# Turning the mixer's activations by DMA instead of on TensorE: six of eight batches of an attention and token/channel-mixer kernel on Trainium2

## The chip, the cores and the metric

The kernel runs on one core of one Trainium2 chip. The metric is the device time of one launch in microseconds (us), the median over the runs shown. The profile is one execution taken by the hardware profiler; its rows name the engines PE (TensorE matmul), PEld (TensorE weight load), DVE (VectorE), ACT (ScalarE), POOL (GpSimd) and SP (SyncE, which here issues most DMAs).

## The reference, cut to what matters

Eight batches, eight heads, 576 tokens of 64 channels per head. Heads 0 to 3 attend to the last 32 tokens, heads 4 to 7 to every fourth of the last 128. The heads' outputs, side by side, are the 576 x 512 matrix x of a batch. It is mixed along the tokens, added to itself, and mixed along the channels:

```python
scores = scale * np.matmul(q, k.transpose(0, 1, 3, 2))
scores = np.where(masks, scores, -1e9)
attn = softmax(scores)
x = heads_side_by_side(np.matmul(attn, v))
h = np.maximum(x.transpose(0, 2, 1) @ w_tok1, 0.0) @ w_tok2
u = x + h.transpose(0, 2, 1)
h2 = np.maximum(u @ w_ch1, 0.0) @ w_ch2
out = u + h2
```

The channel product `u @ w_ch1` sums over the 512 channels, so on TensorE u must lie with its channels on the partitions, while it is computed with its tokens there. u therefore has to be turned over: four channel blocks (cb) of 128, each 128 channels by 576 tokens.

## The kernel before, in words

All matmuls are in fp16. The order of the work is written by hand. `gen_main(b)` is the trunk of batch b: first the channel product `gp` (line 602: 12 row blocks x 2 token halves x 4 channel blocks, in the order 2, 0, 3, 1 of `CBS`, 288 columns each, with a relu into `gt`), then the output product `yp` (line 619: token blocks s = 0 to 3 of 128, each in two column halves of 12 matmuls with 256 columns). After each `yp` block VectorE adds u and writes `o32` (line 629), and SP stores it. Odd batches have one more block (line 639), the last 64 tokens ("the tail") of the batch and of the one before it. `gp` and `yp` share three PSUM banks in turn.

Between the pieces of the trunk of batch b, `interleave` puts the steps that prepare batches b+1 and b+2. Each step has a place on a clock that the generator keeps: every piece of the trunk and every step advances it by a number written beside it (0.65 for half a `yp` column half, 0.28 for one channel block turned over), and a step is emitted once the clock has passed its place. So a step with a later place comes later on every engine, and a step that is taken out lets more of the trunk go ahead of the steps behind it.

For batch b+1 the steps are `value_steps` (attention times values into `xn`), then `mix_steps`: `emit_h1`, `emit_u` (the second token product; VectorE adds `xn` to it and writes u in fp16 as `u16`, line 518, and the tail as `u16t`, line 528) and `emit_uT`. `emit_uT` (lines 530 to 551) turns one channel block: five TensorE transposes (four token blocks and the tail, lines 540, 542, 548, 549) into a PSUM bank, and one copy of 128 x 576 to the tile `uT`, by VectorE or ScalarE. Channel blocks 2 and 3 belong to the dilated heads, whose tokens lie sorted by their remainder of 4; there the copy also puts them back in natural order.

For batch b+2 the steps are casts by GpSimd (`cast_steps`), DMA transposes of q and k (`dma_steps`, line 336) and the copies of the turned blocks to their places (`place_steps`: `plain` on GpSimd, lines 358 and 360; `tails`, `dil` and `dil_k` on VectorE, lines 354, 355, 364, 369), and `score_steps`. For each of four pairs of heads `score_steps` emits three groups of score matmuls into the banks `sc`, `sc` and `sm`, with ScalarE's exponentials; then GpSimd multiplies the results by the mask, in a wide and a narrow product per pair (`mult`, line 113: `attp` for the two plain pairs, `attd` for the two dilated ones).

Every engine works through its own list in order, and SP through its list of DMAs. Below, "the hand-over into batch b" is the moment at which TensorE goes from the last `yp` matmul of batch b-1 to the first `gp` matmul of batch b.

Of the kernel before, what the change touches and what calls it, by code (L numbers as in the profile page):

```python
# [9 lines left out]
FP16 = mybir.dt.float16  # L10
FP32 = mybir.dt.float32
AF = mybir.ActivationFunctionType
ALU = mybir.AluOpType
# [3 lines left out]
S = 576  # L17
# [3 lines left out]
DM = 512  # L21
# [16 lines left out]
CBS = (2, 0, 3, 1)  # L38
# [31 lines left out]
def kernel(  # L70
# [11 lines left out]
    nc = tc.nc  # L82
# [4 lines left out]
    def fixed(name, shape, dtype=FP16):  # L87
        return sb.tile(shape, dtype, tag=name, bufs=1, name=name)
# [29 lines left out]
    ident = const[:, 0:128]  # L118
# [33 lines left out]
    w4 = [w4a[:, i] for i in range(NMB)]  # L152
    idle = fixed("idle", [128, 512])

    def emit_fixed():
# [346 lines left out]
    def emit_u(b, s, h1):  # L502
        p = bank("fl", 3, f"up_{b}_{s}")
        if s < 4:
            summed = b == 1 and s in (0, 2)
            for half in range(2):
                c = slice(256 * half, 256 * half + 256)
                if summed:
                    nc.tensor.matmul(out=p[:, c], lhsT=ident, rhs=xn[b][:, s, c], start=True, stop=False)
                for jb in range(2):  # L510
                    nc.tensor.matmul(  # L511
                        out=p[:, c], lhsT=w2p[jb][:, s] if half else w2[jb][:, 128 * s:128 * s + 128],
                        rhs=h1[jb][:, c], start=(jb == 0 and not summed), stop=(jb == 1))
            t = sb.tile([128, DM], FP16, tag="u16", bufs=8, name=f"u16_{b}_{s}")
            if summed:
                nc.scalar.copy(out=t, in_=p)
            else:
                nc.vector.tensor_tensor(out=t, in0=p, in1=xn[b][:, s], op=ALU.add)  # L518
            u16[(b, s)] = t
        else:  # L520
            odd = b % 2
            c0 = 448 if odd else 512
            for jb in range(2):
                nc.tensor.matmul(out=p, lhsT=w2[jb][:, c0:c0 + 128], rhs=h1[jb],  # L524
                                 start=(jb == 0), stop=(jb == 1))
            rows = slice(64, 128) if odd else slice(0, 64)
            t = u16t[b // 2]
            nc.vector.tensor_tensor(out=t[rows], in0=p[rows], in1=xn[b][rows, 4], op=ALU.add)

    def emit_uT(b, cb):  # L530
        odd = b % 2
        c = slice(128 * cb, 128 * cb + 128)
        p = bank("fl" if b or cb % 2 == 0 else "main", 3, f"tpu_{b}_{cb}", FP16)
        tl = u16t[b // 2][:, c]
        t = sb.tile([128, S], FP16, tag="ut", bufs=5, name=f"uT_{b}_{cb}")
        eng = nc.scalar if cb == 2 or (b and cb == 3) else nc.vector
        if cb < 2:
            m0, t0, c0 = (128, 0, 64) if odd else (0, 512, 0)
            for s in range(4):
                nc.tensor.transpose(out=p[:, m0 + 128 * s:m0 + 128 * s + 128],  # L540
                                    in_=u16[(b, s)][:, c], identity=ident)
            nc.tensor.transpose(out=p[:, t0:t0 + 128], in_=tl, identity=ident)
            copy(eng, t, p[:, c0:c0 + S])
        else:
            grid = p[:, 0:4 * RS].rearrange("p (r i) -> p r i", i=RS)
            m0, t0, c0 = (32, 0, 16) if odd else (0, 128, 0)
            for s in range(4):
                nc.tensor.transpose(out=grid[:, s, m0:m0 + 128], in_=u16[(b, s)][:, c], identity=ident)  # L548
# [27 lines left out]
    def mix_steps(b, t_h1, t_h1b, t_u, t_uT, du=1.0):  # L576
        if b % 2 == 0 and b // 2 not in u16t:
            u16t[b // 2] = sb.tile([128, DM], FP16, tag="u16t", bufs=2, name=f"u16t_{b // 2}")
        h1 = [sb.tile([128, DM], FP16, tag="h1", bufs=4, name=f"h1_{b}_{jb}") for jb in range(2)]
        steps = []  # L580
        for half, at in ((0, t_h1), (1, t_h1b)):
            for jb in range(2):
                steps.append((at + 0.9 * jb, 0.55, lambda jb=jb, half=half: emit_h1(b, jb, half, h1[jb])))
        for i, s in enumerate((4, 0, 1, 2, 3)):
            steps.append((t_u + du * i, 0.44, lambda s=s: emit_u(b, s, h1)))
        for i, cb in enumerate(CBS):
            steps.append((t_uT + 0.9 * i, 0.28, lambda cb=cb: emit_uT(b, cb)))
        return steps

    def gen_main(b):  # L590
# [18 lines left out]
        for s in ((4, 0, 1, 2, 3) if odd else (0, 1, 2, 3)):  # L609
            p = bank("main", 3, f"yp_{b}_{s}")  # L610
            o32 = sb.tile([128, DM], FP32, tag="o32", bufs=4, name=f"o32_{b}_{s}")
            if s < 4:
                for half in range(2):
# [12 lines left out]
                    if last and s == 3:  # L626
                        nc.vector.tensor_tensor(out=o32[:, c], in0=p[:, c], in1=u16[(b, s)][:, c], op=ALU.add)
                    elif half:
                        nc.vector.tensor_tensor(out=o32, in0=p, in1=u16[(b, s)], op=ALU.add)  # L629
                    if half or (last and s == 3):  # L630
# [6 lines left out]
            else:  # L637
                for mb in range(NMB):
                    nc.tensor.matmul(out=p, lhsT=gt[(b // 2, mb)][:, 512:640], rhs=w4[mb],  # L639
                                     start=(mb == 0), stop=(mb == NMB - 1))  # L640
                    if mb in (3, 7):
                        yield 0.87
                nc.vector.tensor_tensor(out=o32, in0=p, in1=u16t[b // 2], op=ALU.add)
                nc.sync.dma_start(out=out[b - 1, 512:S, :], in_=o32[0:64])
# [41 lines left out]

    u16t[0] = sb.tile([128, DM], FP16, tag="u16t", bufs=2, name="u16t_0")

    def gate(t, src):
# [31 lines left out]
    nc.gpsimd.memset(u16t[0][64:128], 0.0)  # L721

# [50 lines left out]
    h1 = [sb.tile([128, DM], FP16, tag="h1", bufs=4, name=f"h1_0_{jb}") for jb in range(2)]  # L773
    for s in range(4):
        u16[(0, s)] = sb.tile([128, DM], FP16, tag="u16", bufs=8, name=f"u16_0_{s}")

    def u_half(s, half):
        p = bank("main" if half else "fl", 3, f"up_0_{s}_{half}")[:, 0:256]
        c = slice(256 * half, 256 * half + 256)
        rows = slice(0, 64) if s == 4 else slice(0, 128)  # L780
        t = u16t[0] if s == 4 else u16[(0, s)]
        summed = s in (0, 2)
# [6 lines left out]
        if summed:  # L789
            nc.scalar.copy(out=t[:, c], in_=p)  # L790
        else:
            nc.vector.tensor_tensor(out=t[rows, c], in0=p[rows], in1=xn[0][rows, s, c], op=ALU.add)

# [42 lines left out]
    for b in range(B):  # L836
# [64 lines left out]
```

## Time and profile before

| | |
|---|---|
| median of 3 runs | 300.8 us (300.75 to 302.64) |
| the profiled execution: its own time | 300.74 us |
| the profiled execution: span of the profile | 298.7 us |
| granted TensorE clock, mean | 0.997 |
| PE busy | 286.8 us, 3112 matmuls |
| DVE / ACT / POOL busy | 159.3 / 140.8 / 180.1 us |

The span runs from the first to the last instruction of the profile; what lies around it is the other 2.0 us of the execution's time. Busy time is the time in which an engine has an instruction under way. A number in square brackets in the timeline is idle time ahead of an instruction, with what ended it.

### The profile page before, as it was taken

To read this page: it belongs to the slowest core of one execution; us is meant where nothing else is said; L and a number is where in the kernel's file an instruction comes from. 1 tells how busy PE (TensorE), PEld (TensorE's weight loads), DVE (VectorE), ACT (ScalarE), POOL (GpSimd) and SP (SyncE) were. 2 spreads that over 40 slices of the span, in tenths; PEclk is the share of its full clock that TensorE was granted. 3 is DMA by queue.
4 is the path that set the end of the run, shared out by engine and by line. 5 is a ranking of instruction groups with operands and counts; after the bars stand their busy time and mean duration, and the time that the engine had idled before them with its cause. 6 is when DMAs were issued, how large, how long until landed. Compare 5 with 4: busy or idle time off the path is not lost.

```text
span 298.7 us, 7805 instructions
## 1 busy us (share of the span) xinstructions
PE 286.8 (96%) x3112; PEld 257.2 (86%) x3112; DVE 159.3 (53%) x357; ACT 140.8 (47%) x319; POOL 180.1 (60%) x244
## 2 busy tenths in 40 slices
PE   5789999998999999999999999999999999999995
PEld 2687999987987999899987999899988999899794
DVE  5875438756737965643645254644745264532122
ACT  2853436377652545455545536365554535304500
POOL 7882056429998899739992999449992930000000
PEclk9999999999999999999999999999999999999998
DMA  7999999966997999984599749964551220022023
GB/s 219 270 212 177 214 312 222 326 165 188 286 196 128 279 288 154 280 211 151 69 205 276 211 111 153 307 139 146 120 55 35 72 72 0 3 71 72 2 70 105
DMA packets 91443, 49.10 MB, mean 164 GB/s; under 512 B 59760, under 2 KB 90352, under 8 KB 91408
## 3 DMA queue, kind: packets, MB, share of 16 engines
q1 hardware_dynamic: 87168, 43.53, 59.7%
q0 software_dynamic: 2640, 3.91, 7.4%
q10 hardware_dynamic: 1600, 1.18, 1.3%
q8 instruction: 24, 0.39, 0.6%
q14 instruction: 11, 0.09, 0.1%
HBM read 37.04 MB, written 9.44 MB: 156 GB/s over the span
## 4 chain that ended last, share of the span: by engine, by line
PE 92%; DVE 3%; DMA 2%; ACT 1%; issue 1%; ACTq 0%; POOLq 0%
PE gp L602 31%; PE yp L619 28%; PE sc L393 4%; PE h1p L499 4%; PE up L511 4%; PE yp L639 3%; DMA const<-consts 2%; PE sm L393 1%; PE tpu L548 1%; PE av L469 1%; PE h1p L497 1%; PE av L480 1%; PE tpu L540 1%; PE up L524 1%; PE av L467 1%; PE sc L391 1%
## 5 line engine op out<-in xcount | busy, mean ns | idle before, releaser
L602 PE MATMUL gp<-uT,w 128*128 128x288 f16 x768 | 109.9, 286 | 0.7 <-ACT uT L101 0.6
L619 PE MATMUL yp<-w,gt 128*128 128x256 f16 x756 | 95.6, 273 | 0.0
L107 ACT ACTIVATE gt<-gp 128x288 f16<-128x288 f32 x138 | 56.6, 410 | 72.1 <-PE gp L602 65.9
L602 PEld LDWEIGHTS <-w 128*128 128x128 f16 x768 | 83.1, 113 | 8.2 <-issue 1.2
L619 PEld LDWEIGHTS <-gt 128*128 128x128 f16 x768 | 75.9, 106 | 3.7
L113 POOL TENSOR_TENSOR attp<-attp,const 128x1280 f16<-128x1280 f16 (+1 forms) x24 | 36.0, 1529 | 32.9 <-ACT attp L422 32.9
L629 DVE TENSOR_TENSOR o<-yp,u 128x512 f32<-128x512 f32 x31 | 21.3, 689 | 50.6 <-PE yp L619 44.2
L109 DVE TENSOR_SCALAR gt<-gp 128x288 f16<-128x288 f32 x54 | 24.6, 455 | 35.5 <-PE gp L602 33.5
L113 POOL TENSOR_TENSOR attd<-attd,const 128x1024 f16<-128x1024 f16 (+1 forms) x24 | 32.8, 1397 | 0.0
L113 DVE TENSOR_TENSOR xn<-av,rec 128x320 f16<-128x320 f32 x64 | 31.5, 491 | 2.2
L393 PEld LDWEIGHTS <-kt 128*128 128x128 f16 x272 | 22.5, 101 | 3.1 <-DVE kt L302 1.6
L103 POOL CAST c_q<-l_q 128x512 f16<-128x512 f32 x31 | 18.9, 613 | 6.4 <-DMA l_q<-in_q_dram 5.7
L413 ACT ACTIVATE attp<-sc 128x480 f16<-128x480 f32 x32 | 18.0, 572 | 9.5 <-PE sc L393 9.4
L518 DVE TENSOR_TENSOR u<-up,xn 128x512 f16<-128x512 f32 x26 | 17.9, 691 | 8.0 <-PE up L511 8.0
L360 POOL COPY qz<-qt 64x512 f16<-64x512 f16 x20 | 21.4, 1072 | 0.6
L442 ACT ACTIVATE attd<-sc 128x512 f16<-128x512 f32 x32 | 18.9, 597 | 5.3 <-PE sc L393 4.7
L488 DVE RECIPROCAL rec<-av 128x5 f32<-128x5 f32 x64 | 12.2, 191 | 14.3 <-PE av L475 7.2
L393 PE MATMUL sc<-qz,kt 128*128 128x160 f16 (+1 forms) x144 | 18.6, 228 | 1.3 <-DVE kt L302 1.3
L103 POOL CAST c_k<-l_k 128x512 f16<-128x512 f32 x29 | 18.0, 622 | 3.0 <-DMA l_k<-in_k_dram 1.3
L101 ACT COPY uT<-tpu 128x576 f16<-128x576 f16 x15 | 9.6, 640 | 16.3 <-PE tpu L549 16.3
L107 ACT ACTIVATE h<-h1p 128x256 f16<-128x256 f32 x28 | 10.7, 383 | 10.1 <-PE h1p L499 8.0
L639 PE MATMUL yp<-w,gt 128*128 128x512 f16 x48 | 12.0, 379 | 0.0
(131 smaller groups left out, 444.4 us busy)
## 6 DMA issues: line engine op xcount, KB each, us to landing
out_dram<-o SPq DMA_DIRECT2D x72, 128.0 KB, 2.5
l_q<-in_q_dram SPq DMA_DIRECT2D x15, 512.0 KB, 6.4
l_k<-in_k_dram SPq DMA_DIRECT2D x14, 512.0 KB, 7.4
l_vn<-in_v_dram SPq DMA_DIRECT2D x32, 128.0 KB, 6.7
l_vd<-in_v_dram SPq DMA_DIRECT2D x16, 256.0 KB, 3.9
w<-in_moe_w_ch_dram POOLq DMA_DIRECT2D x6, 512.0 KB, 7.6
lt<-in_q_dram SPq DMA_DIRECT2D x8, 128.0 KB, 4.4
l_vt<-in_v_dram SPq DMA_DIRECT2D x8, 128.0 KB, 4.3
```

What stands on the lines that cost most here:

```text
L103: eng.tensor_copy(out=out, in_=in_)
L107: nc.scalar.activation(out=out, in_=in_, func=AF.Relu)
L109: eng.tensor_scalar_max(out=out, in0=in_, scalar1=0.0)
L113: eng.tensor_tensor(out=out, in0=x, in1=y, op=ALU.mult)
L360: nc.gpsimd.tensor_copy(out=natural(qz[hp][halves[h], h, 0:512]), in_=qta[halves[h], hp].rearrange("p r m -> p m r"))
L393: nc.tensor.matmul(out=out, lhsT=lhsT, rhs=qz[hp][:, h, queries], start=hide is None, stop=True)
L413: nc.scalar.activation(out=blocks[:, h, 0:3, 0:BLK], in_=p[:, 0:3 * BLK].rearrange("p (b c) -> p b c", c=BLK), func=AF.Exp, scale=0.125)
L442: nc.scalar.activation(out=a[:, h, 0:DTL], in_=p, func=AF.Exp, scale=0.125)
L602: nc.tensor.matmul(out=p[:, 0:288], lhsT=w3[cb][:, 512 * (mb // 4) + mb % 4:512 * (mb // 4) + 512:4], rhs=uT[(b, cb)][:, 288 * sh:288 * sh ...
L619: nc.tensor.matmul(out=p[:, c], lhsT=gt[(b // 2, mb)][:, a0:m0 + 512:4] if half else gt[(b // 2, mb)][:, a0:a0 + 128], rhs=w4[mb][:, c], s ...
L629: nc.vector.tensor_tensor(out=o32, in0=p, in1=u16[(b, s)], op=ALU.add)
L639: nc.tensor.matmul(out=p, lhsT=gt[(b // 2, mb)][:, 512:640], rhs=w4[mb], start=(mb == 0), stop=(mb == NMB - 1))
```

## The change

From batch 2 on, u is no longer turned on TensorE. u of a batch is written into one tile of 128 x (4 channel blocks, 4 token blocks, 128). Two DMA transposes on SP's list turn it: the tail (4 blocks of 128 x 128, into `uTt`) and the four token blocks (16 blocks, into `uTm`), placed at 2.0 and 6.0 after the batch's first step of u. Then four VectorE copies bring the turned blocks into the tile `uTd` that `gp` reads: the tail of all channel blocks; channel block 2, whose tokens are read with a stride to put them in natural order; channel blocks 0 and 1 in one copy; and channel block 3, strided as well. They are placed 0.9 apart from 28.4 on (29.6 for batch 2), where the turning on TensorE began at 18.2 (22.2). Neither the DMA steps nor the copies advance the generator's clock. Batches 0 and 1 keep `emit_uT`. `uTm`, `uTt` and `uTd` are one buffer each, and GpSimd zeroes the second half of both tail tiles at the start instead of one. The views `u16(b, s)` and `blocks4` only reshape the operands of the other instructions.

```diff
+    uTm = fixed("utm", [128, 4, 4, 128])
+    uTt = fixed("utt", [128, 4, 128])
+    uTd = fixed("utd", [128, 4, S])
...
-    xn, u16, u16t, uT, gt = {}, {}, {}, {}, {}
+    xn, u16w, uT, gt = {}, {}, {}, {}
+    u16t = [fixed(f"u16t{i}", [128, 4, 128]) for i in range(2)] * 2
+
+    def u16(b, s):
+        if b not in u16w:
+            u16w[b] = sb.tile([128, 4, 4, 128], FP16, tag="u16", bufs=2, name=f"u16_{b}")
+        return u16w[b][:, :, s]
...
-            t = sb.tile([128, DM], FP16, tag="u16", bufs=8, name=f"u16_{b}_{s}")
             if summed:
-                nc.scalar.copy(out=t, in_=p)
+                nc.scalar.copy(out=u16(b, s), in_=blocks4(p))
             else:
-                nc.vector.tensor_tensor(out=t, in0=p, in1=xn[b][:, s], op=ALU.add)
-            u16[(b, s)] = t
+                nc.vector.tensor_tensor(out=u16(b, s), in0=blocks4(p), in1=blocks4(xn[b][:, s]), op=ALU.add)
...
+    def turned(b):
+        return b >= 2
+
+    def uT_dma(b, tail):
+        if tail:
+            nc.sync.dma_start_transpose(out=uTt, in_=u16t[b // 2].rearrange("p x c -> p (x c)"))
+        else:
+            nc.sync.dma_start_transpose(out=uTm.rearrange("p x s t -> p (x s) t"),
+                                        in_=u16w[b].rearrange("p x s c -> p (x s c)"))
+
+    def uT_place(b, i):
+        r0, m0, t0 = (64, 64, 0) if b % 2 else (0, 0, 512)
+        if i == 0:
+            for cb in range(4):
+                uT[(b, cb)] = uTd[:, cb]
+            nc.vector.tensor_copy(out=uTd[:, :, t0:t0 + 64], in_=uTt[:, :, r0:r0 + 64])
+        elif i == 1:
+            nc.vector.tensor_copy(out=uTd[:, 0:2, m0:m0 + 512], in_=uTm[:, 0:2].rearrange("p x s t -> p x (s t)"))
+        else:
+            nc.vector.tensor_copy(out=natural(uTd[:, i, m0:m0 + 512]), in_=uTm[:, i].rearrange("p r m -> p m r"))
...
-        for i, cb in enumerate(CBS):
-            steps.append((t_uT + 0.9 * i, 0.28, lambda cb=cb: emit_uT(b, cb)))
+        if turned(b):
+            for t, tail in ((2.0, True), (6.0, False)):
+                steps.append((t_u + t * du, 0.0, lambda tail=tail: uT_dma(b, tail)))
+            for i, x in enumerate((0, 2, 1, 3)):
+                steps.append((t_uT + 0.9 * i, 0.0, lambda x=x: uT_place(b, x)))
+        else:
+            for i, cb in enumerate(CBS):
+                steps.append((t_uT + 0.9 * i, 0.28, lambda cb=cb: emit_uT(b, cb)))
...
-            steps += mix_steps(2, 10.8, 14.6, 17.2, 22.2)
+            steps += mix_steps(2, 10.8, 14.6, 17.2, 29.6)
...
-                steps += value_steps(b + 1, 0.6, 1.1) + mix_steps(b + 1, 6.6, 10.6, 13.2, 18.2)
+                steps += value_steps(b + 1, 0.6, 1.1) + mix_steps(b + 1, 6.6, 10.6, 13.2, 28.4)
```

VectorE's list ahead of the hand-over into batch 3, before. `o32_2_s` is the output add of token block s of batch 2, `uT_3` the turned u of batch 3, `gt_0` the first relu of batch 3:

```order
L103 COPY uT_3_0_2456<-tpu_3_0_2455 128x576
L629 TENSOR_TENSOR o32_2_0_2429<-yp_2_0_2428,u16_2_0_1769 128x512
L103 COPY uT_3_1_2489<-tpu_3_1_2488 128x576
L629 TENSOR_TENSOR o32_2_1_2504<-yp_2_1_2503,u16_2_1_1783 128x512
L629 TENSOR_TENSOR o32_2_2_2564<-yp_2_2_2563,u16_2_2_1796 128x512
L629 TENSOR_TENSOR o32_2_3_2614<-yp_2_3_2613,u16_2_3_1814 128x512
```

The same place in the changed kernel (`utt`, `utm` and `utd` are the tiles `uTt`, `uTm` and `uTd`):

```order
L663 TENSOR_TENSOR o32_2_1_2433<-yp_2_1_2432,u16_2_1767 128x512
L663 TENSOR_TENSOR o32_2_2_2489<-yp_2_2_2488,u16_2_1767 128x512
L578 COPY utd_89<-utt_88 128x4x64
L582 COPY utd_89<-utm_87 128x512
L663 TENSOR_TENSOR o32_2_3_2544<-yp_2_3_2543,u16_2_1767 128x512
L580 COPY utd_89<-utm_87 128x2x512
L582 COPY utd_89<-utm_87 128x512
```

Two of the four copies now stand behind the add of the last token block, which needs the last `yp` of batch 2; the hand-over into batch 5 reads the same. The hand-overs into 4 and 6, here into 4, have the last two copies ahead of that add:

```order
L663 TENSOR_TENSOR o32_3_1_3034<-yp_3_1_3033,u16_3_2337 128x512
L578 COPY utd_89<-utt_88 128x4x64
L582 COPY utd_89<-utm_87 128x512
L663 TENSOR_TENSOR o32_3_2_3089<-yp_3_2_3088,u16_3_2337 128x512
L580 COPY utd_89<-utm_87 128x2x512
L582 COPY utd_89<-utm_87 128x512
L663 TENSOR_TENSOR o32_3_3_3147<-yp_3_3_3146,u16_3_2337 128x512
```

So has the one into batch 2, except that there the add of block 2 stands between the copy of channel blocks 0 and 1 and that of block 3. Into batch 7 all four copies stand behind the last add:

```order
L663 TENSOR_TENSOR o32_6_2_4673<-yp_6_2_4672,u16_6_4030 128x512
L663 TENSOR_TENSOR o32_6_3_4702<-yp_6_3_4701,u16_6_4030 128x512
L578 COPY utd_89<-utt_88 128x4x64
L582 COPY utd_89<-utm_87 128x512
L580 COPY utd_89<-utm_87 128x2x512
L582 COPY utd_89<-utm_87 128x512
```

Nothing stands between the last of these copies and the first relu of batch 7. On SP's list the large transpose of batch 3 comes behind the first load of v for batch 5:

```order
L191 DMA l_q_5_0_2315<-in_q_dram 128x4x256
L568 DMA_TRANSPOSE utt_88<-u16t1_91 128x4x128
L191 DMA l_k_5_0_2317<-in_k_dram 128x4x256
L191 DMA l_q_5_1_2316<-in_q_dram 128x4x256
L191 DMA l_k_5_1_2318<-in_k_dram 128x4x256
L208 DMA l_vn_5_2403<-in_v_dram 128x4x64
L570 DMA_TRANSPOSE utm_87<-u16_3_2337 128x16x128
L208 DMA l_vn_5_2403<-in_v_dram 128x4x64
```

Before, neither transpose stood there; the loads followed one another.

More of the change, by code (lines that the diff above doesn't have):

```diff
@@ L642, in gen_main @@
                         yield 0.87
[L643 removed]
+                nc.vector.tensor_tensor(out=blocks4(o32), in0=blocks4(p), in1=u16t[b // 2], op=ALU.add)
                 nc.sync.dma_start(out=out[b - 1, 512:S, :], in_=o32[0:64])
@@ L720 @@
             out=w2p[jb], in_=w2[jb][:, 0:512].rearrange("p (m r) -> p r m", r=4))
-    nc.gpsimd.memset(u16t[0][64:128], 0.0)
+    for i in range(2):
+        nc.gpsimd.memset(u16t[i][64:128], 0.0)
     warm(8)
@@ L789, in u_half @@
         if summed:
-            nc.scalar.copy(out=t[:, c], in_=p)
+            nc.scalar.copy(out=t, in_=blocks4(p))
         else:
-            nc.vector.tensor_tensor(out=t[rows, c], in0=p[rows], in1=xn[0][rows, s, c], op=ALU.add)
+            nc.vector.tensor_tensor(out=t[rows], in0=blocks4(p[rows]), in1=blocks4(xn[0][rows, s, c]), op=ALU.add)
     for jb in range(2):
```

22 lines of the change are left out of this document (9 added, 13 removed).

## The prediction

> **What bounds the kernel now.** I read the page first, then the windows between hand-overs, then the chain of waits.
>
> ```profile
> span 298.7 us, 7805 instructions
> PE 286.8 (96%) x3112; PEld 257.2 (86%) x3112; DVE 159.3 (53%) x357; ACT 140.8 (47%) x319; POOL 180.1 (60%) x244
> ```
>
> ```profile
> core 0: us, PE busy (x) PEld busy (x) DVE busy (x) ACT busy (x) POOL busy (x), PEclk, DMA share, GB/s
> ...
> 107.13:139.21 32.08, 32.08 (x357) 29.64 (x356) 16.60 (x40) 16.35 (x37) 25.04 (x31) 1.00 0.91 217
> 139.21:173.72 34.51, 34.51 (x372) 30.82 (x369) 17.27 (x41) 17.11 (x39) 28.73 (x34) 1.00 0.74 181
> ...
> 240.30:270.10 29.80, 29.80 (x313) 27.46 (x312) 14.83 (x33) 10.19 (x24) 1.30 (x2) 1.00 0.11 37
> ```
>
> The windows begin and end at hand-overs (into 2 at 107.13, into 3 at 139.21, into 4 at 173.72, into 7 at 270.1). From one to the next TensorE is busy for the whole window (32.08 of 32.08 us) at full clock, and no other engine is. So a matmul taken out there is worth its time, and every wait that TensorE gets is lost in full. The chain gives TensorE's pace:
>
> ```profile
> 262.33 7.86 PE yp L619 x72
> 270.19 11.76 PE gp L602 x96
> ```
>
> That is 0.109 us per `yp` matmul and 0.1225 per `gp` matmul.
>
> **What the change removes.** The timeline of TensorE around the turning of batch 3:
>
> ```profile
> 126.19 0.82 PE L619 MATMUL yp<-w,gt 128*128 128x256 f16 x6
> 126.85 0.39 PE L540 MATMUL tpu<-const,u 128*128 128x128 f16 x4
> 127.07 0.22 PE L542 MATMUL tpu<-const,u16t 128*128 128x128 f16 x1
> 127.13 0.82 PE L619 MATMUL yp<-w,gt 128*128 128x256 f16 x6
> ```
>
> From one `yp` group to the next are 0.94 us; the six `yp` matmuls take 0.655, so five transposes take 0.285, though each row shows 0.22 or more (matmuls overlap). Four blocks in six batches: 24 x 0.285 = **6.8 us** off TensorE. The copies out of PSUM that go too (two on DVE, two on ACT per batch) bring nothing, since neither engine bounds.
>
> **What it adds: copies between two SBUF tiles on VectorE.** The kernel has such copies already, in the same forms: line 364 dense, line 355 the tail, line 369 read with the stride. By line or tile, min/median/max, then the timelines of VectorE and GpSimd where the maxima lie:
>
> ```profile
> L364 DVE COPY qz<-qt x10: 407/416/2729, 98.1 to 228.8; 64x1024 f16<-64x1024 f16 x10
> L369 DVE COPY kt<-kr x10: 263/272/2685, 101.3 to 229.4; 128x128 f16<-128x128 f16 x10
> L355 DVE COPY kt<-tt x5: 226/226/977, 94.4 to 225.1; 128x256 f16<-128x256 f16 x5
> ```
>
> ```profile
> 98.10 3.17 DVE L364 COPY qz<-qt 64x1024 f16<-64x1024 f16 x2
> 101.30 2.99 DVE L369 COPY kt<-kr 128x128 f16<-128x128 f16 x2
> 104.20 1.27 DVE L629 TENSOR_TENSOR o<-yp,u 128x512 f32<-128x512 f32 x2
> ```
>
> ```profile
> 98.33 6.25 POOL L113 TENSOR_TENSOR attp<-attp,const 128x1280 f16<-128x1280 f16 x4 [1.94 <-ACT attp L422]
> 104.54 5.47 POOL L113 TENSOR_TENSOR attd<-attd,const 128x1024 f16<-128x1024 f16 x4
> ```
>
> ```profile
> L113 POOL TENSOR_TENSOR attp<-attp,const 128x1280 f16<-128x1280 f16 x12 | 31.4, 2615 | 32.9 <-ACT attp L422 32.9
> L113 POOL TENSOR_TENSOR attd<-attd,const 128x1024 f16<-128x1024 f16 x12 | 25.5, 2126 | 0.0
> ```
>
> This decides the case. The second copy of line 364 takes 2.73 us instead of 0.42, the second of line 369 2.69 instead of 0.27: each begins while GpSimd is in a wide mask product (2.615) and ends just behind it. The first pair ends at 98.10 + 3.17 = 101.27, the product at 98.33 + 2.62 = 100.95. The output adds, which read PSUM and one SBUF tile, run beside the same products at their usual 0.64 each (1.27 for two). So an SBUF copy waits out the GpSimd instruction it meets, GpSimd's next one starts behind it, and the following copy waits for that. Behind such a wait a copy costs 0.32, 0.10 less than alone.
>
> Prices behind a wait: the tail 0.226 - 0.10 = 0.13; the dense copy 0.32. A strided copy of 512 is not in the trace. Lines 355 and 364 (0.226 for 256, 0.416 for 1024) give a fixed 0.165; line 369 leaves 0.107 for 128, so 0.165 + 4 x 0.107 = 0.59, behind a wait 0.49. Its bounds are 0.19 (at line 364's rate) and 0.59 (the whole 0.685 of line 302, the same shape out of PSUM, less 0.10). I take 0.49, since line 369 has the same pattern.
>
> ```profile
> L302 DVE COPY kt<-tp_k 128x512 f16<-128x512 f16 x12 | 8.1, 685 | 2.4 <-PE tp_k L297 2.4
> ```
>
> Where GpSimd is at each hand-over:
>
> ```profile
> 131.76 5.96 POOL L113 TENSOR_TENSOR attp<-attp,const 128x1280 f16<-128x1280 f16 x4 [6.86 <-ACT attp L422]
> 137.68 5.47 POOL L113 TENSOR_TENSOR attd<-attd,const 128x1024 f16<-128x1024 f16 x4
> ```
>
> ```profile
> 139.21 1.15 PE L602 MATMUL gp<-uT,w 128*128 128x288 f16 x8
> ```
>
> ```profile
> 139.29 0.69 DVE L629 TENSOR_TENSOR o<-yp,u 128x512 f32<-128x512 f32 x1 [2.49 <-PE yp L619]
> ```
>
> ```profile
> 163.65 5.94 POOL L113 TENSOR_TENSOR attp<-attp,const 128x1280 f16<-128x1280 f16 x4 [5.60 <-ACT attp L422]
> ```
>
> ```profile
> 236.13 5.46 POOL L113 TENSOR_TENSOR attd<-attd,const 128x1024 f16<-128x1024 f16 x4
> ```
>
> At every hand-over but the last, GpSimd is in its mask series: from 131.76 to 143.15 around 139.21, from 163.65 around 173.72, from 98.33 around 107.13; into 7 it has been idle since 241.6. The series: wide 2.57, narrow 0.41, wide 2.57, narrow 0.41 (5.96), then 2.09, 0.63, 2.09, 0.63 (5.44), from the means less 0.04 of overlap. It follows the scores. The removed steps had advanced the generator's clock by 4 x 0.28 = 1.12; now two more `yp` groups of six (1.31 us) go ahead of the scores, so the series begins 1.31 later against the hand-over: 7.49 us ahead into 2, 6.14 into 3 and 5, 8.76 into 4 and 6.
>
> **The stalls, step by step.** Zero is the hand-over without a stall; an output add starts 0.21 behind its last matmul, as above (139.29 against a `yp` that ends 0.13 ahead of 139.21, four small score matmuls lying between).
>
> Into 3 (and 5): the add of block 2 ends at -2.95. The tail meets the second wide product, which ends at -0.52, and ends at -0.39. Channel block 2 waits for the narrow product (0.02) and ends at 0.51. The last output add runs 0.51 to 1.12. Now the copy of blocks 0 and 1 waits for the product begun at 0.51, until 2.60, and ends at 2.92; block 3 waits 0.63 more and ends at 4.04. `gp` takes its blocks in the order 2, 0, 3, 1, so it runs two matmuls early and goes on at 4.1: **3.8 us** lost, twice.
>
> Into 4 (and 6): the tail ends at -3.01, block 2 at -2.11, blocks 0 and 1 at 0.30, block 3 at 1.42: **1.2 us**, twice.
>
> Into 2: two copies of line 369 come ahead and wait as well; the tail ends at -1.43, block 2 at -0.53, blocks 0 and 1 at 1.88, then the add of block 2, then block 3 at 3.00: **2.8 us**.
>
> Into 7: no product in the way, but all four copies behind the last add (0.21 to 0.82): 2.25, **2.1 us**.
>
> Sum: 2.8 + 3.8 + 1.2 + 3.8 + 1.2 + 2.1 = 14.9 lost, 6.8 won: +8.1. The span goes from 298.7 to 306.8, the execution from 300.7 (the median is 300.8) to **308.8 us**. With the strided copy at its bounds the stalls sum to 11.6 and 16.2: 305.5 and 310.1.
>
> **The DMA transposes.** They need SP's time and must land.
>
> ```profile
> qt<-c_q SPq DMA_TRANSPOSE x10, 3.5
> kr<-c_k SPq DMA_TRANSPOSE x10, 3.8
> tt<-c_t SPq DMA_TRANSPOSE x5, 2.5
> ```
>
> ```profile
> L336 SPq DMA_TRANSPOSE kr<-c_k x10: 1267/1286/2066, 85.1 to 216.1; - x10
> ...
> DMA to landing us min/median/max: 3.2/3.8/5.0
> ```
>
> Four blocks land in 2.5 us, eight in 3.5 to 3.8, so sixteen in some 5.5 to 6; the bounds are 3.2 (eight at best) and twice the worst, 10. The issue of eight takes 1.3 to 2.1; sixteen 1.3 to 4. Block 3 of u is added some 12 us ahead of the hand-over into 3, and the tail's turn comes at -2.95: 9 us. What is queued behind the large transpose on SP are loads of v for batch b+3, which are cast a whole trunk later, and output stores; neither is waited for soon. I cost this at nothing; at the worst it adds 1 to 2 us where loads are in front, into 2.
>
> [...] The second copy of line 369 moved 128 elements per partition in 0.107 us, 1.2 per ns, where line 364 moves 4 per ns, and yet it took 2.69 us beside the product. [...]
>
> **The rivals.** *Strided copies pass freely*: block 2 and block 3 do not wait for GpSimd, only the tail and the dense copy do. The same walk gives 2.4, 2.8, 0.2, 2.8, 0.2 and 2.2: 10.6 lost, +3.8, **304.5**. [...] Against: 2685 ns.
>
> *No copy meets GpSimd* (the other side): the waits at 98 to 104 are those of one hand-over, and if the products stood elsewhere only VectorE's order would cost: into 3 and 5 the add (0.82), the dense copy (1.24) and the strided one (1.73) give 1.4 each, into 7 2.1, the others nothing. 4.9 - 6.8 = -1.9: **298.8**. It decides once all stalls stay under 6.8. Against: the series is driven by the scores, and its place follows from the order.
>
> *Full gain*: no stall at all, **294**. Against: into 7 the copies stand behind the last add whatever GpSimd does.
>
> *A cold TensorE*: the first matmuls run slowly, the same shape taking 580 against 379 ns:
>
> ```profile
> L667 PE MATMUL idle_p<-idle 128*128 128x512 f16 x10 | 4.2, 580 | 2.5 <-POOL idle L156 2.5
> L639 PE MATMUL yp<-w,gt 128*128 128x512 f16 x48 | 12.0, 379 | 0.0
> ```
>
> If a stall of 3.8 us brought that back for as long as there (some 4.2 us at half speed), each would cost 2.1 more, into 3 and 5: **313**. [...] Against it: two `gp` matmuls break the stall into pieces under 2.5 us.
>
> **How the numbers follow.** My forecast, copies that wait, 0.70, alone 305 to 312. Strided copies free 0.08, no copy meets GpSimd 0.09, full gain 0.04, cold TensorE or late transposes 0.09. The range is 303 to 313: it takes in the first rival and leaves out some 0.18. A change within 1% (297.8 to 303.8) is about what a measurement cannot tell from none. Faster by more: the full gain, 0.04. Within: 0.10. Slower: 0.86.
>
> **What would show it.** Right: no `tpu` rows from batch 2 on, TensorE idle ahead of `gp` at six hand-overs with VectorE's `uTd` copies as releasers, 3 to 4 us into 3 and 5 and about 1 into 4 and 6; dense copies of over 2 us beside GpSimd's products; a gap into 7 of about 2 with short copies. Wrong: copies near 0.4 at all hand-overs, or gaps that end with a DMA.

## The result and the profile after

| | before | after |
|---|---|---|
| median | 301.36 us (300.75 to 302.64, 4 runs) | 312.81 us (310.98 to 313.43, 4 runs) |
| profiled execution, its own time / span | 300.74 / 298.7 us | 312.23 / 310.3 us |
| granted TensorE clock, mean | 0.997 | 0.983 |

The change makes the kernel slower: ratio 1.0364, 95% interval 1.0303 to 1.0425. The forecast was 308.8 us, with a range of 303 to 313: the result lies 4.0 us above the forecast and 0.2 below the top of the range.

The page, its first line and the line of busy times:

```profile
span 310.3 us, 7572 instructions
PE 286.6 (92%) x2992; PEld 252.9 (81%) x2992; DVE 182.8 (59%) x369; ACT 132.8 (43%) x307; POOL 185.6 (60%) x245
```

TensorE has 120 instructions fewer, and yet its busy time is what it was (286.8 before): 6.6 us of work went (experiment 3), and what is left took longer; the clock in the windows below is the main reason. VectorE is busy 23.5 us more. The windows from hand-over to hand-over (into 2 at 105.99, into 3 at 144.24, and so on to the one into 7):

```profile
105.99:144.24 38.25, 34.28 (x339) 30.03 (x337) 23.30 (x44) 14.84 (x36) 26.24 (x32) 0.91 0.99 214
144.24:182.15 37.91, 35.22 (x346) 30.34 (x346) 23.79 (x45) 16.19 (x38) 29.35 (x33) 0.95 0.75 187
182.15:214.12 31.97, 31.26 (x336) 28.66 (x335) 19.66 (x42) 14.59 (x35) 24.87 (x31) 1.00 0.76 189
214.12:250.58 36.46, 33.78 (x346) 29.71 (x346) 23.65 (x45) 16.17 (x38) 29.39 (x33) 1.00 0.53 119
```

The first column behind the times is the length of the window, the second TensorE's busy time; the seventh is the granted clock. Before, the two were equal and the clock 1.00. Now 4.0, 2.7, 0.7 and 2.7 us are missing from TensorE, and the clock is at 0.91 and 0.95 in the trunks of batches 2 and 3. The waits of TensorE, by what ended them, in us, times, and the longest:

```profile
PE gp L636 <- DVE utd L582: 6.9, 7, 2.8
PE gp L636 <- DVE utd L580: 5.0, 3, 2.0
```

No gap ahead of `gp` ends with a DMA. The copies themselves, min/median/max in ns:

```profile
L582 DVE COPY utd<-utm x12: 584/850/2525, 104.2 to 281.6; 128x512 f16<-128x512 f16 x12
L578 DVE COPY utd<-utt x6: 217/2455/2639, 101.6 to 280.6; 128x256 f16<-128x256 f16 x6
L580 DVE COPY utd<-utm x6: 418/1752/2354, 105.0 to 281.2; 128x1024 f16<-128x1024 f16 x6
```

The minima are those of the hand-over into 7, where GpSimd has nothing to do; a strided copy alone takes 0.584 us. The maxima stand beside mask products. The hand-over into 2 at 105.99, VectorE and then GpSimd:

```profile
101.63 2.64 DVE L578 COPY utd<-utt 128x256 f16<-128x256 f16 x1
104.19 0.86 DVE L582 COPY utd<-utm 128x512 f16<-128x512 f16 x1
104.96 2.35 DVE L580 COPY utd<-utm 128x1024 f16<-128x1024 f16 x1
107.24 0.68 DVE L663 TENSOR_TENSOR o<-yp,u 128x512 f32<-128x512 f32 x1
107.84 2.52 DVE L582 COPY utd<-utm 128x512 f16<-128x512 f16 x1
```

```profile
98.55 6.02 POOL L113 TENSOR_TENSOR attp<-attp,const 128x1280 f16<-128x1280 f16 x4 [2.08 <-ACT attp L434]
104.53 6.37 POOL L113 TENSOR_TENSOR attd<-attd,const 128x1024 f16<-128x1024 f16 x4
```

Each copy begins while a product is under way and ends just behind it, and the next product lasts longer by about what is left of the copy (the wide one begun at 104.53 takes 2.50 us, where such products took 2.13 before): the two engines take turns, one instruction each. The add at 107.24 keeps its 0.68. It lets GpSimd get through a narrow product and begin the next wide one (in the single records at 107.81, ending at 109.92), so the last copy, begun at 107.84, waits out a wide product as well. TensorE at the hand-overs into 2 and 3, and then into 5:

```profile
106.00 0.29 PE L636 MATMUL gp<-utd,w 128*128 128x288 f16 x1
107.37 0.28 PE L636 MATMUL gp<-utd,w 128*128 128x288 f16 x1 [1.08 <-DVE utd L580]
110.42 0.88 PE L636 MATMUL gp<-utd,w 128*128 128x288 f16 x3 [2.77 <-DVE utd L582]
...
146.51 0.28 PE L636 MATMUL gp<-utd,w 128*128 128x288 f16 x1 [1.98 <-DVE utd L580]
147.49 1.60 PE L636 MATMUL gp<-utd,w 128*128 128x288 f16 x6 [0.69 <-DVE utd L582]
...
216.39 0.28 PE L636 MATMUL gp<-utd,w 128*128 128x288 f16 x1 [1.99 <-DVE utd L580]
217.37 0.90 PE L636 MATMUL gp<-utd,w 128*128 128x288 f16 x6 [0.69 <-DVE utd L582]
```

The first matmul has its block in time, the second waits for blocks 0 and 1, the third for block 3, as forecast. The last four rows show something else. Into 3 and into 5 the waits are equal (1.98 and 0.69, 1.99 and 0.69), but behind them six matmuls take 1.60 us into 3 and 0.90 into 5. The windows say why (the column behind the busy times is the granted clock):

```profile
106.20:109.61 3.41, 0.37 (x2) 0.11 (x1) 3.41 (x3) 0.38 (x1) 3.41 (x3) 1.00 0.99 269
143.75:147.16 3.41, 0.93 (x11) 0.52 (x8) 3.41 (x4) 0.91 (x3) 3.41 (x3) 1.00 0.91 267
147.16:150.57 3.41, 3.08 (x23) 2.18 (x23) 1.42 (x4) 0.41 (x1) 3.41 (x4) 0.50 0.33 110
212.02:215.43 3.41, 2.24 (x27) 1.97 (x25) 3.41 (x4) 1.85 (x4) 3.41 (x3) 1.00 0.59 137
215.43:218.84 3.41, 1.76 (x20) 1.49 (x20) 2.42 (x4) 0.41 (x1) 3.41 (x3) 1.00 0.88 263
```

From 109.61 to 116.44 and from 147.16 to 150.57, behind the hand-overs into 2 and 3, TensorE runs at half its clock (0.50); behind the one into 5 it does not. These borders lie a whole number of 3.41 us apart: 6.83 is two of them, 30.72 is nine. The changes of the clock in the profiles of the experiments lie so too: in experiment 1 those at 143.65 and 211.91 are 68.26 apart, twenty times 3.41, in experiment 8 those at 141.52 and 213.20 are 71.68 apart, twenty-one times. So the rows above are cut along this grid. Into 2 and into 3 one window has TensorE idle for 3.04 and 2.48 us (its length less the busy time), and the clock is halved from its end on. Into 5 nearly the same waits lie across a border, with 1.17 us in one window and 1.65 in the next, and the clock stays at 1.00. The profiles of the experiments bear this out: between the hand-overs there are eleven windows, with those of this kernel, behind which the clock falls, and TensorE is idle in each for 1.84 us or more; in no window behind which it stays at 1.00 is TensorE idle for more than 1.74 us. The halving lasts for one such window each time, but for two into 2 here.

The idle time was not one gap: no wait here is longer than 2.77 us, and 1.84 us in one window were enough (experiment 1).

### The profile page after: what moved, and what is told of

The parts are those of the page before. It is cut to its first block, busy times and chain, and to the rows that moved or that the text cites. A ratio compares the mean times of both kernels' runs of the same rounds, so it can differ in the third digit from the quotient of the medians.

```text
span 310.3 us, 7572 instructions
## 1 busy us (share of the span) xinstructions
PE 286.6 (92%) x2992; PEld 252.9 (81%) x2992; DVE 182.8 (59%) x369; ACT 132.8 (43%) x307; POOL 185.6 (60%) x245
## 4 chain that ended last, share of the span: by engine, by line
PE 78%; DVE 15%; DMA 2%; issue 2%; ACT 1%; SPq 0%; DVEq 0%; ACTq 0%; POOLq 0%
PE gp L636 31%; PE yp L653 19%; PE h1p L511 4%; PE up L523 4%; DVE utd L578 4%; DVE utd L582 3%; PE yp L673 3%; DVE utd L580 3%; PE sc L405 3%; DMA const<-consts 2%; DVE o L663 2%; PE av L481 1%; PE h1p L509 1%; PE av L492 1%; PE av L479 1%
## 5 line engine op out<-in xcount | busy, mean ns | idle before, releaser
L636 PEld LDWEIGHTS <-w 128*128 128x128 f16 x768 | 84.0, 115 | 23.9 <-issue 13.9
L636 PE MATMUL gp<-utd,w 128*128 128x288 f16 x576 | 88.2, 294 | 12.3 <-DVE utd L582 6.9
L653 PE MATMUL yp<-w,gt 128*128 128x256 f16 x756 | 93.1, 273 | 0.0
L113 POOL TENSOR_TENSOR attd<-attd,const 128x1024 f16<-128x1024 f16 (+1 forms) x24 | 37.4, 1586 | 0.0
L425 ACT ACTIVATE attp<-sc 128x480 f16<-128x480 f32 x32 | 17.2, 571 | 26.6 <-PE sc L405 26.5
L636 PE MATMUL gp<-uT,w 128*128 128x288 f16 x192 | 26.8, 286 | 0.7 <-ACT uT L101 0.6
L405 PEld LDWEIGHTS <-kt 128*128 128x128 f16 x272 | 22.2, 101 | 3.4 <-DVE kt L314 1.6
L405 PE MATMUL sc<-qz,kt 128*128 128x160 f16 (+1 forms) x144 | 17.7, 229 | 1.2 <-DVE kt L314 1.2
L481 PE MATMUL av<-vv,attp 128*128 128x65 f16 x128 | 12.7, 201 | 0.0
```

The lines of the kernel that those rows point to most:

```text
L113: eng.tensor_tensor(out=out, in0=x, in1=y, op=ALU.mult)
L405: nc.tensor.matmul(out=out, lhsT=lhsT, rhs=qz[hp][:, h, queries], start=hide is None, stop=True)
L425: nc.scalar.activation(out=blocks[:, h, 0:3, 0:BLK], in_=p[:, 0:3 * BLK].rearrange("p (b c) -> p b c", c=BLK), func=AF.Exp, scale=0.125)
L636: nc.tensor.matmul(out=p[:, 0:288], lhsT=w3[cb][:, 512 * (mb // 4) + mb % 4:512 * (mb // 4) + 512:4], rhs=uT[(b, cb)][:, 288 * sh:288 * sh ...
L653: nc.tensor.matmul(out=p[:, c], lhsT=gt[(b // 2, mb)][:, a0:m0 + 512:4] if half else gt[(b // 2, mb)][:, a0:a0 + 128], rhs=w4[mb][:, c], s ...
```

## The experiments

The theory: the removal is worth 6.8 us, the transposes by DMA cost nothing by themselves, the VectorE copies cost because they wait out GpSimd's instructions, and a cold TensorE comes on top. The rivals: the copies stand too late in VectorE's list and nothing else is wrong (order); the transposes are late (DMA). The time before, measured again beside each group of runs below, was 300.8 to 301.6 us.

**1. The copies on ScalarE.**

```diff
-            nc.vector.tensor_copy(out=uTd[:, :, t0:t0 + 64], in_=uTt[:, :, r0:r0 + 64])
+            nc.scalar.copy(out=uTd[:, :, t0:t0 + 64], in_=uTt[:, :, r0:r0 + 64])
...
```

(likewise the other three)

> The four copies per batch go to ScalarE, at the same places in the order; nothing else changes. Theory (VectorE's SBUF copies wait out GpSimd's mask products and stand behind the output adds; the slow clock follows from those stalls): ScalarE waits for neither, so the gaps into 2, 4, 6 and 7 go, into 3 and 5 some 1.8 us each stay because the last two copies stand behind an exponential of the last score bank there (exponential to 0.55, dense copy about 1.0, strided 0.64). 6.8 won, 3.6 lost: about 297.5, no clock dip. Rival (the large DMA transpose is late, 6.3 us to land and up to 5.8 us of SP's time): the gaps stay, whoever copies, 308 or more, and they end with a DMA.

Measured: 305.32 us (304.63 to 306.81, 4 runs), ratio 1.0158 (1.0113 to 1.0202). It is 7.5 us under the changed kernel, but 7.8 above the 297.5 expected. No copy waits for GpSimd any more; they have other prices:

```profile
103.23 1.06 ACT L582 COPY utd<-utm 128x512 f16<-128x512 f16 x1 [2.28 <-DMA utm<-u]
104.20 1.08 ACT L454 ACTIVATE attd<-sc 128x512 f16<-128x512 f32 x2
```

```profile
PE sm L405 <- ACT attd L454: 2.1, 3, 1.5
...
PE sc L405 <- ACT attd L462: 1.5, 1, 1.5
```

A strided copy takes ScalarE 1.06 us, and into 2 it stands 2.28 us at the head of ScalarE's list until the large transpose has landed at 103.2; the exponentials behind it come late, and TensorE waits for those. So the transpose into 2 is later than the prediction had it (its 9 us of room were worked out for the hand-over into 3), and an engine with work for TensorE behind the copy passes the lateness on. Into 3 and 5 the last copies stand behind an exponential, as expected, and the third `gp` matmul is 2.0 us late at each (1.8 expected). The miss has two parts: the lateness into 2, which makes the trunk of batch 1 longer than in experiment 3 by 3.3 us, and a halved clock that was not expected, from 143.65 to 147.06 and from 211.91 to 215.33, behind the waits into 3 and 5. Against experiment 3 the trunks of batches 3 and 5 are some 3.6 us longer each, of which 2.0 is the stall.

**2. No mask products from batch 3 on.**

```diff
-        if not veils:
+        if not veils and b < 3:
             mult(nc.gpsimd, blocks[:, :, :, 0:BLK], blocks[:, :, :, 0:BLK], band)
...
-        if not veils:
+        if not veils and b < 3:
             mult(nc.gpsimd, diag, diag, band[:, :, :, 0:128])
```

> GpSimd's mask products are left out from batch 3 on (the scores of batches 3 to 7 are not masked); the copies stay on VectorE. Theory: copies run at 0.22, 0.42 and 0.59 everywhere, and only VectorE's order is left: into 3 and 5 some 1.4 us each, into 7 2.1, the others nothing, 298.8, no clock dip. If VectorE's order were the whole cause: gaps as now, 312. If the transposes were late: gaps as now, ending with a DMA.

Measured: 298.86 us (one run), span 297.0. The copies in the same places:

```profile
L582 DVE COPY utd<-utm x12: 575/598/618, 103.4 to 268.2; 128x512 f16<-128x512 f16 x12
L578 DVE COPY utd<-utt x6: 216/218/266, 100.4 to 267.2; 128x256 f16<-128x256 f16 x6
L580 DVE COPY utd<-utm x6: 418/418/591, 103.9 to 267.9; 128x1024 f16<-128x1024 f16 x6
```

With the same order and no product to meet, every copy takes its own time, the clock stays at 1.00, and 13.3 us of span go. That is what the meeting costs, the cold TensorE that follows it included. What order alone costs is left: 297.0 against the 292.1 of the next run, 4.9 us.

**3. No copies.** `gp` of batches 2 to 7 reads 288 columns of `uTm` as they lie.

```diff
-                        rhs=uT[(b, cb)][:, 288 * sh:288 * sh + 288], start=(cb == order[0]), stop=(cb == order[-1]))
+                        rhs=uT[(b, cb)][:, (224 if turned(b) else 288) * sh:(224 if turned(b) else 288) * sh + 288], start=(cb == order[0]), stop=(cb == order[-1]))
```

> No copies: the channel product of batches 2 to 7 reads the tile that the large DMA transpose writes (columns 0 to 287 and 224 to 511; the tail is left out and the tokens are not put in order), so the matmuls, the transposes and the wait for them are as in the changed kernel. Theory: the full 6.8 us, 294, no gap at a hand-over, no clock dip. If the transposes were late: gaps of over 1 us that end with a DMA, 296 or more. If the DMA traffic slowed the rest: more than 296 without gaps.

Measured: 293.88 us (one run), span 292.1. Its window from the hand-over into 2 to that into 3:

```profile
105.99:137.43 31.44, 31.10 (x339) 28.68 (x337) 19.12 (x39) 15.02 (x36) 25.53 (x32) 1.00 0.99 228
```

The transposes run as in the changed kernel, with one wait of 0.3 us for them, into 3. So the removal is worth 298.7 - 292.1 = 6.6 us, and the copies cost 310.3 - 292.1 = 18.2.

**4. Dummy matmuls ahead of `gp`**, so that TensorE does not idle before the hand-overs into 2, 3 and 5; the copies stay.

```diff
+        if b in (2, 3, 5):
+            warm(10)
```

> Ten matmuls of 512 columns on zeros (2.2 us at full clock) ahead of the channel product of batches 2, 3 and 5, where TensorE waits over 3 us; they work on nothing and lie within the wait. Theory (the stalls themselves bring the granted clock down to 0.5 for some us behind the hand-overs into 2 and 3, about 4.5 us in the profiled run): the clock stays at 1.00, the stalls stay, 308. Rival (the lower clock is not what costs, or does not come from idle time): 312, or 314 with the added matmuls.

Measured: 309.47 us (308.26 to 309.78, 4 runs), ratio 1.0272 (1.0235 to 1.0308).

```profile
112.00:114.00 2.00, 2.00 (x17) 1.45 (x16) 1.19 (x4) 0.41 (x1) 2.00 (x5) 0.50 1.03 312
114.00:116.00 2.00, 2.00 (x21) 1.57 (x20) 0.57 (x2) 0.82 (x2) 2.00 (x5) 0.75 1.05 321
...
148.00:152.00 4.00, 4.00 (x60) 3.73 (x59) 3.15 (x10) 2.05 (x5) 4.00 (x8) 1.00 0.28 74
```

The `gp` matmuls wait for the same copies, but from 148 to 152 the clock is 1.00, where it was 0.68 in the changed kernel, and the span is 2.5 us shorter (307.8 for 310.3). Into 2 a wait of 1.86 us was left behind the dummies, and behind it the clock still fell, now for 3.41 us instead of 6.83. In the other three of the four runs the mean clock is 1.00, at spans of 306.4 to 307.9. The time lies 1.5 us above the theory's 308 and under the rival's 312, so the cold running is a cost of its own, beside the stalls.

**5. The copies 2.4 places earlier**, to tell the wait for GpSimd from mere order.

```diff
-            steps += mix_steps(2, 10.8, 14.6, 17.2, 29.6)
+            steps += mix_steps(2, 10.8, 14.6, 17.2, 27.2)
...
-                steps += value_steps(b + 1, 0.6, 1.1) + mix_steps(b + 1, 6.6, 10.6, 13.2, 28.4)
+                steps += value_steps(b + 1, 0.6, 1.1) + mix_steps(b + 1, 6.6, 10.6, 13.2, 26.0)
```

> The four VectorE copies are placed 2.4 earlier on the generator's clock: into 3 and 5 all of them now stand ahead of the last output add, into 4 and 6 one block earlier too, into 7 two of the four ahead of it. Theory (each copy waits out the GpSimd product it meets): the copies only meet other products; into 3 and 5 the last strided copy still waits for the first dilated product and ends some 3.3 us behind the hand-over, so stalls of 3.0 there, about 4 into 2, 0.5 into 4 and 6, 1.4 into 7, with clock dips 305 to 310. Rival (what costs is that copies stand behind the last output add): nothing is left into 2 to 6, 1.4 into 7, 296 to 298, no dip.

Measured: 308.75 us (307.86 to 309.63, 2 runs), ratio 1.0241 (1.0194 to 1.0289). VectorE ahead of the hand-over into 3, here at 142.15, and GpSimd there:

```profile
139.21 2.82 DVE L582 COPY utd<-utm 128x512 f16<-128x512 f16 x1
141.94 0.66 DVE L580 COPY utd<-utm 128x1024 f16<-128x1024 f16 x1
142.52 2.50 DVE L582 COPY utd<-utm 128x512 f16<-128x512 f16 x1
```

```profile
135.91 6.41 POOL L113 TENSOR_TENSOR attp<-attp,const 128x1280 f16<-128x1280 f16 x4 [7.49 <-ACT attp L434]
142.28 5.99 POOL L113 TENSOR_TENSOR attd<-attd,const 128x1024 f16<-128x1024 f16 x4
```

All copies stand ahead of the last add now, and still the last one ends 2.9 us behind the hand-over, since each takes its turn with a product. The order-only rival (296 to 298) falls. The clock halved three times. Into 2 the gap only moved: the copies of `kt` stood behind a copy that waited for the large transpose, and TensorE's scores waited 3.6 us for `kt`.

**6. The channel product reads the transposed tiles where they lie**, channel blocks 2 and 3 with a stride of 128 elements, the tail by matmuls of 64 columns.

```diff
+            return uTm[:, cb].rearrange("p r m -> p m r")[:, c0 // 4:(c0 + n) // 4]
...
+                for c0, c1, rhs in pieces(b, sh):
+                    for cb in order:
```

> No copies and nothing left out: the channel product of batches 2 to 7 reads the tiles that the DMA transposes write, channel blocks 2 and 3 with the stride that puts the tokens in order; the half that holds the tail is two products per channel block (224 and 64 columns). Theory: TensorE's moving operand does not meet GpSimd, so no stall and no clock dip; the split adds 4 x (0.0958 + 0.0325 - 0.1225) = 0.02 us in each of 72 banks, 1.7 us in all: 295.5, faster than before by 1.7%. Rival (a strided moving operand runs slower): the strided matmuls take more than 0.1225 us each; at half speed 288 of them cost 35 us, 330.

What it changes of the computation: the single tail tile is written again by a later transpose before the last row blocks are through (that of batch 4 lands at 185.7, and batch 3 reads the tile until 185.9), so some of their tail columns come out wrong. Measured: 391.93 us (390.7 to 393.41, 6 runs), ratio 1.3004 (1.2965 to 1.3042). That is 96 us above the theory, and 62 above the rival with half speed. The groups, with mean ns:

```profile
L645 PE MATMUL gp<-utm,w 128*128 128x288 f16 x288 | 100.0, 477 | 0.0
...
L645 PE MATMUL gp<-utm,w 128*128 128x224 f16 x288 | 80.8, 410 | 0.0
```

Busy TensorE is 376.3 us against 286.8. Half of the `utm` rows are dense and half strided; in the single records a strided one of 288 columns begins 0.48 us ahead of the next, a dense one 0.1225. That the strided pattern sets this price, four times the dense one, is shown; why TensorE slows so was not tried.

**7. Half by DMA.** Only channel blocks 0 and 1 are transposed by DMA, straight into the tile that `gp` reads (two tiles in turn); blocks 2 and 3, the strided ones, stay on TensorE.

```diff
+    uTd = [fixed(f"utd{i}", [128, 2, 640]) for i in range(2)]
...
+        nc.sync.dma_start_transpose(out=d[:, x, m0:m0 + 512].rearrange("p (s t) -> p s t", t=128),
+                                    in_=u16w[b][:, x].rearrange("p s c -> p (s c)"))
...
+            if cb >= 2 or not turned(b):
+                steps.append((t_uT + 0.9 * i, 0.28, lambda cb=cb: emit_uT(b, cb)))
```

> Only the channel blocks 0 and 1 of u of batches 2 to 7 come by DMA, and they land where the channel product reads them (two tiles in turn), so that nothing is copied; blocks 2 and 3 stay transposes on TensorE with their VectorE evictions as before. Nothing of the computation is left out. Theory (the port waits and the clock dip that follows them are all that the change costs): ten transposes of 0.0555 us a batch leave TensorE, 3.4 us in all, no hand-over into a batch waits, so about 297.4 us (296.5 to 298.5). Rival (the DMA transposes are late by themselves, the first batch's above all): a gap at the head of gp ends with a DMA and the time is 299 us or more.

Measured: 297.1 us (296.72 to 297.75, 6 runs), ratio 0.9869 (0.9839 to 0.9900), as the theory had it: 1.0 to 1.6% less than the kernel before. What the expectation calls port waits are the times for which the copies stood beside GpSimd's products, up to 2.64 us each in the changed kernel; that a port is the cause was not shown.

```profile
106.76:138.28 31.52, 31.52 (x346) 29.11 (x345) 17.42 (x38) 16.17 (x37) 24.91 (x31) 1.00 0.98 217
138.28:172.24 33.96, 33.96 (x361) 30.29 (x359) 17.00 (x39) 17.24 (x40) 28.70 (x34) 1.00 0.91 210
```

TensorE is busy throughout again, at full clock, in windows that are 0.55 us shorter than before: ten transposes of 0.0555.

**8. The strided copies on GpSimd**, ahead of its masks; everything else by DMA in place.

```diff
+        nc.gpsimd.tensor_copy(out=natural(uTd[b % 2][:, x, m0:m0 + 512]),
+                              in_=uTm[:, x - 2].rearrange("p r m -> p m r"))
```

> All four channel blocks and the tail come by DMA; blocks 0 and 1 and the tail land where the channel product reads them, without a copy, and the two strided copies of blocks 2 and 3 run on GpSimd just ahead of its mask series, where it is idle in batches 2 to 6. Nothing of the computation is left out. Theory (the copies cost only because VectorE's meet GpSimd's instructions): with no copy left on VectorE the whole removal of 6.8 us is kept, 294 to 295 us. Rival (the transposes are too late for copies this early): GpSimd waits at the head of its series for a DMA, the masks come late, gaps stand at av or gp, and the time is 298 us or more.

Measured: 307.1 us (303.97 to 308.12, 6 runs), ratio 1.0184 (1.0139 to 1.0229). The rival was right; the clock halved twice on top, from 141.52 and from 213.20 on. GpSimd into 3, SP's issue there, and TensorE's longest group of waits:

```profile
137.03 2.09 POOL L584 COPY utd<-utm 128x512 f16<-128x512 f16 x2 [7.29 <-DMA utm<-u]
```

```profile
128.28 4.87 SPq L575 DMA_TRANSPOSE utm<-u  x1
```

```profile
PE av L480 <- POOL attp L113: 3.1, 3, 1.7
```

Issued at 128.28, the transpose had landed at 137.03, 1.3 us ahead of the hand-over at 138.29: room for a copy that nothing waits behind, none for one at the head of the mask series.

**9 and 10. The strided copies on ScalarE**, both (9), or only that of block 2, with block 3 on TensorE (10); the rest by DMA in place.

```diff
+        nc.scalar.copy(out=natural(uTd[b % 2][:, x, m0:m0 + 512]),
+                       in_=uTm[:, x - 2].rearrange("p r m -> p m r"))
```

> Blocks 0, 1 and the tail land by DMA where the channel product reads them, blocks 2 and 3 land in a small tile, their transpose the first on the queue, and ScalarE makes the two strided copies just ahead of the hand-over; the channel product takes the blocks in the order 0, 1, 2, 3. Nothing of the computation is left out. Theory (no copy on VectorE, so none meets GpSimd; the masks are not behind a copy as in the run with GpSimd's copies): the 6.8 us are won, less what 2.1 us on ScalarE a batch delay: the transpose of batch 3 landed 1.3 us ahead of the hand-over in that run, so some 0.5 to 1 us at the hand-overs into 3 and 5, 295 to 296.5 us. Rival (ScalarE waits for the DMA and the exps queue behind it, as with all four copies on ScalarE): 300 us or more.

> Blocks 0, 1 and 2 of batches 2 to 7 come by DMA, block 3 stays a TensorE transpose with its ScalarE eviction; blocks 0, 1 and the tail land in place, block 2 in a small tile, and ScalarE makes one strided copy just ahead of the hand-over; the channel product takes block 2 last. Nothing of the computation is left out. Theory: 15 transposes of 0.0555 us a batch are won, 5.0 us in all, the one copy of 1.06 us is done before block 2 is read, about 296 us (295 to 297). Rival (the wait for the DMA blocks ScalarE's queue): 298.5 us or more, above the half that stays on TensorE.

Measured: 298.1 us (297.57 to 300.28, 9 runs), ratio 0.9911 (0.9880 to 0.9942), for two; 297.65 us (296.53 to 297.98, 6 runs), ratio 0.9859 (0.9826 to 0.9893), for one. Both beat the kernel before, by 0.9 and 1.4%, and both are above what the theory gave (295 to 296.5, and 295 to 297). ScalarE with two, into 3, and what TensorE waited for:

```profile
136.57 1.07 ACT L584 COPY utd<-utm 128x512 f16<-128x512 f16 x1 [1.33 <-DMA utm<-u]
137.54 0.38 ACT L461 ACTIVATE attd<-sm 128x256 f16<-128x256 f32 x1
137.82 1.06 ACT L584 COPY utd<-utm 128x512 f16<-128x512 f16 x1
```

```profile
PE sm L404 <- ACT attd L453: 2.7, 4, 1.1
```

As in 1, the exponentials behind the copies come late, now by about 1 us at a time. This profile is that of the slowest of the nine runs (300.28 us), and the clock halved once in it (from 139.29 on), so the median run may wait less. With one copy the same wait is 0.5 us in all, so of the 5.0 us won some 4 remain. Its interval and that of the half overlap; the half is the simpler kernel.

## Why the prediction was right, and where it was not

The length of each trunk in us, from hand-over to hand-over (the last to the end of the span):

| trunk of batch | before | after | no masks (2) | no copies (3) | half (7) |
|---|---|---|---|---|---|
| 1 | 37.32 | 36.16 | 36.17 | 36.17 | 36.72 |
| 2 | 32.08 | 38.25 | 31.72 | 31.44 | 31.53 |
| 3 | 34.51 | 37.91 | 34.68 | 33.46 | 33.96 |
| 4 | 32.07 | 31.96 | 30.92 | 30.92 | 31.52 |
| 5 | 34.51 | 36.46 | 34.64 | 33.47 | 33.96 |
| 6 | 29.72 | 30.77 | 30.05 | 28.47 | 29.17 |
| 7 | 28.7 | 28.9 | 29.0 | 28.3 | 28.6 |

*The removal*: forecast 6.8, measured 6.6 (experiment 3).

*The copies wait for GpSimd*: right, and shown by 2 and 5. The strided copy alone takes 0.584 (forecast 0.59), and beside a product 2.52, so the rival in which it passes freely falls. What the runs show is one instruction at a time (2.64, 0.86, 2.35 and 2.52 us for the copies into 2, where they take 0.22, 0.58, 0.42 and 0.59 into 7), with the output adds, which read one SBUF input, unaffected at 0.68; why the two engines take turns was not tried.

*The stalls*: by how late the third `gp` matmul starts (into 7 with the 1.6 us by which the first is late against experiment 3), they are 4.2, 3.0, 0.7, 3.0, 0.7 and 2.2, against the forecast 2.8, 3.8, 1.2, 3.8, 1.2 and 2.1: 13.8 for 14.9. Into 2 the walk let the last copy meet the narrow product; the add ahead of it gave GpSimd the time to begin a wide one, 1.4 us more. Into 3 and 5 the series stood a little further ahead (137.71, 6.53 ahead of 144.24, forecast 6.14).

*The cold TensorE* is the step that failed. The prediction set it as a rival at 0.09, against its own stalls, though it has the stalls for its cause and can only come with them; and it argued that two `gp` matmuls break the stall into harmless pieces. Pieces were enough: 1.08 and 2.77 us into 2, 1.98 and 0.69 into 3, since what goes with the fall of the clock is the idle time within one window of 3.41 us, not one unbroken gap. Against experiment 3 the trunk of batch 2 is longer by 6.8, of which 4.2 is the stall, and that of batch 3 by 4.45, of which 3.0 is the stall: 2.6 and 1.5, together 4.1 us. (TensorE is at work for 6.0 and 3.1 us of the time at half clock, and half of that gives nearly the same, 3.0 and 1.5.) The rival's price, 2.1 a dip and 4.2 in all, was about right, but it had the dips into 3 and 5, and they came into 2 and 3. Then 13.8 + 4.1, and 0.3 of small waits ahead of the hand-overs, are the 18.2 of the copies, and 18.2 - 6.6 = 11.6 is the span's growth from 298.7 to 310.3. Without the dips the forecast of +8.1 would have stood against +7.5. That the result lies inside the range is in part luck: the theory alone gave 305 to 312, two of the four runs (313.38 and 313.43 us) lie above 313, and whether a stall brings the clock down hangs on where it falls on the grid, as the equal waits into 3 and 5 show (2.48 us idle in one window, against 1.17 and 1.65 in two).

*The transposes at nothing*: right for the changed kernel, where no gap ahead of `gp` ends with a DMA, and yet thinner than it was told. Their issue on SP took more than the bound of 4, and they landed in 6.3 us where 5.5 to 6 had been estimated:

```profile
L570 SPq DMA_TRANSPOSE utm<-u x6: 1757/4148/5843, 97.9 to 270.2; - x6
...
DMA to landing us min/median/max: 4.3/6.3/8.3
```

Experiments 1, 5, 8 and 9 all meet it: an engine that comes to its copy sooner runs into the landing. Into 2 a copy waits for it until 103.23 in 1 and 103.40 in 5, and in the changed kernel the first copy that reads it begins at 104.19: about 1 us of room. The longer issue times come where loads stand in front on SP (3.65 to 5.84 us for batches 2 to 5, against 1.76 and 1.88 for 6 and 7); whether those loads are the cause was not tried.

*The other side* (298.8 if no copy meets GpSimd) gave the right price for its case, 298.86 in experiment 2; its condition did not hold here.

## What to carry to other kernels

Work taken off the bounding engine is won only if nothing that replaces it stands between two of its instructions: the 6.6 us were there, and four copies per batch of 0.2 to 0.6 us gave back 18, of which 13 because they met GpSimd's products. Turn by DMA what can land where it is read, and leave on TensorE what would need another copy. And a stall that is found can have two prices, its own length and the lower clock behind it (here 0.50 for one or two windows of 3.41 us, behind 1.84 us or more of idle time in one window): where it is near 2 us or longer, put both into the sum, instead of setting the second as a rival against the first.

## What the runs showed of the hardware that was not expected

- A moving operand read with a stride of 128 fp16 elements costs TensorE 0.48 us per 288 columns instead of 0.1225 (experiment 6).
- A DMA transpose of sixteen blocks holds SP for 1.8 to 5.8 us (median 4.1) and lands 4.3 to 8.3 us after its issue.
- In these profiles the granted clock changed on a grid of 3.41 us, between 1.00 and 0.50. Between the hand-overs it was halved behind every window of that length in which TensorE was idle for 1.84 us or more, and behind none with 1.74 or less, so equal waits into 3 and into 5 had different ends.
- A strided SBUF copy of 128 x 512 in fp16 takes ScalarE 1.06 to 1.13 us (experiment 1), VectorE 0.58 alone, GpSimd 1.05 to 1.12 (experiment 8).
